# Linear attention and two squared-ReLU layers on one core: whole-word keys times values for the second token block, and split operands kept in two places

## The chip, the cores and the metric

The kernel runs on one core of a Trainium2 chip. The metric is device time in microseconds (us) of one execution; a median is taken over several.

## The reference

All tensors are float32; 8 batches, 8 heads, 576 positions, 64 values per head, so 4608 tokens of 512 values.

```python
q_s = softmax(q, over the 64 values of a head)
k_s = softmax(k, over the 576 positions)
kv  = einsum('bhsd,bhse->bhde', k_s, v)          # 64 x 64 for each batch and head
x   = einsum('bhsd,bhde->bhse', q_s, kv)         # then 4608 x 512
x   = (relu(x @ w_in)  ** 2) @ w_out             # 512 -> 2048 -> 512
y   = (relu(x @ w_in2) ** 2) @ w_out2            # 512 -> 2048 -> 512
```

## The kernel before, in words

**Tiling.** The tokens are cut into nine blocks of 512 (`j` = 0 to 8), the heads into four pairs (`p` = 0 to 3), the 2048 hidden values into sixteen chunks (`f`). There are four stages: the first layer's first product together with the attention (0 to some 500 us), its second product, and the two products of the second layer. The last three use a scheme with seven block products instead of eight and are not touched.

**Split operands.** Most products run in a reduced type. An operand is split into a high word (a copy by ScalarE) and a low word (operand minus high word, by VectorE), and a product takes three passes: low times high, high times low, high times high (`passes`, line 451; for the attention `x_mm`, line 411). A product in whole words, plain float32, needs no split.

**Attention.** Batches have 576 positions and blocks 512 tokens, so block `j` needs two batches: its first 64 `j` columns belong to batch `j` - 1, the rest to batch `j`. For a pair, keys are exponentiated, `kv_mm` (line 318) multiplies keys and values into the PSUM tile `kvps`, `kv_norm` (line 335) divides into `kvn`. `kv_hi` (line 343, ScalarE) and `kv_lo` (line 348, VectorE) write the two words of the pair's block-diagonal operand into `kvbd`. There is one `kvbd` for each pair, so `x_mm` comes in two parts: part 0 uses the words of batch `j` - 1, then `kv_hi` and `kv_lo` overwrite them, then part 1 uses batch `j`. The queries become probabilities, are transposed by VectorE into `qT` (`q_turn`, line 400) and split into `qhl` (`q_hi`, `q_lo`, lines 404 to 409). The result `xps` is split again into `xs` (`x_hi`, `x_lo`), which the first layer reads.

**Block 0** is the start and goes another way: keys and queries are transposed by TensorE against a unit matrix, `kv_whole0` (line 354) copies `kvn` whole into the tile `begin`, and `x_mm0` (line 295) multiplies in whole words. Batch 0's split words are still made, for block 1.

**Weights.** `first_weights` (line 764) brings in the sixteen weight chunks of the first product: a load, then `low_word`, `high_word`, `scaled` and `join` (lines 144 to 161) turn 64-bit numbers into float32, and `w_hi`, `w_lo` split them. `background` (line 823) converts the other three matrices during the first stage and later, one half chunk at a time, through a single room `qa`, by the same function `converted` (line 741).

**The order of the work** is written out by a planner in the kernel. Each step is an `op` with an engine, a cost in ns, a due time, the steps it follows, and the places (rooms of memory) that it uses. `schedule` (line 614) plays this through: on each engine the ready step with the earliest due time goes next, if its places are free. A place with one slot goes from user to user in the order in which they were written; `kvn`, `qT`, `qd` (which holds `begin`, then each `qhl` in turn) have one slot. `lag` is time added before a step counts as ready after a step of another engine. The instructions are then issued in that order, and each engine works through its own queue in order. `attend` (line 861) writes the steps of a block's attention, `plain_chunk` (line 939) those of a chunk of h.

Of the kernel before, what the change touches and what calls it, by code (L numbers as in the profile page):

```python
# [44 lines left out]
def linear_attention_two_relu2_ffn(ctx: ExitStack, tc: tile.TileContext, q0, k0, eye, qh, kh, vh, wio, out):  # L45
# [171 lines left out]
    kvbd = []  # L217
# [45 lines left out]
    def k_turn0(p, b1, b2):  # L263
        k = kt[0, p]
        a, b = ka[p] = wide(b1, f"ka{p}").rearrange("p (c n) -> p c n", n=P), wide(b2, f"kb{p}")
        for c in range(KC):
            r = slice(c * P, (c + 1) * P) if c < KC - 1 else slice(S - P, S)
            nc.tensor.transpose(a[:, c] if c < KC - 1 else b[:, :P], k[:, r], begin[1])
# [15 lines left out]
    def q_turn0(p, b):  # L284
        q = qt.pop((0, p)).rearrange("p a b -> p (a b)")
        ps = ka[p, "q"] = wide(b, f"qps{p}")
        for c in range(4):
            r = slice(c * P, (c + 1) * P)
            nc.tensor.transpose(ps[:, r], q[:, r], begin[1])
# [5 lines left out]
    def x_mm0(p, b):  # L295
        xps[0, p] = wide(b, f"xps0_{p}")
        nc.tensor.matmul(xps[0, p], begin[0][:, p], qTt.pop((0, p)), start=True, stop=True)
# [44 lines left out]

    def kv_hi(b, p):
        for j in range(2):
            r = slice(j * D, (j + 1) * D)
            nc.scalar.activation(out=kvbd[p][r, 0, r], in_=kvn[b, p][r], func=AF.Copy)

    def kv_lo(b, p):
        n, t = kvn.pop((b, p)), kvbd[p]
        for j in range(2):  # L350
            r = slice(j * D, (j + 1) * D)
            nc.vector.tensor_tensor(out=t[r, 1, r], in0=n[r], in1=f32(t[r, 0, r]), op=ALU.subtract)
# [104 lines left out]

    def filler(place, n):

        ps, z = bank(place, f"filler{place.index}")[:, 0], kvbd[0]  # L460
        for _ in range(n):
            nc.tensor.matmul(ps, z[:, 0], z.rearrange("p a n -> p (a n)"), start=True, stop=True)
# [101 lines left out]
    WORDS = {"qx": 2 * TB, "att1": KC * (P + 2 * (D + 1)), "att2": KC * (P + 2 * (D + 1))}  # L564
# [176 lines left out]
    def converted(f, a, h, due, raw, wf):  # L741
# [3 lines left out]
        c = op("ACT", act(512) + 40, due - 3000, lambda: low_word(f, a, h), [l], [rp])  # L745
        g = op("DVE", 430, due - 2900, lambda: high_word(f, a, h), [l], [rp], port=True)
# [435 lines left out]
```

## Time and profile before

| | us |
|---|---|
| median of 3 runs | 1543.55 (1541.88 to 1543.83) |
| the profiled execution's own time | 1544.59 |
| its span, first to last instruction | 1542.8 |
| TensorE matmuls busy | 1508.4 (98%) |
| VectorE busy | 1166.9 (76%) |
| ScalarE busy | 946.9 (61%) |
| GpSimd busy | 401.6 (26%) |
| mean granted TensorE clock | 0.99 |

In the profile PE is TensorE's matmuls, PEld its weight loads, DVE VectorE, ACT ScalarE, POOL GpSimd, SPq the queue that issues DMAs. On a timeline a row has the start in us, the length in us, the engine, the line, the operation, output <- inputs, shapes and how many instructions are merged; in brackets stands how long the engine had been idle before it, and what it waited for. Matmuls overlap, so lengths of neighbouring rows may add up to more than the time that passed.

### The profile page before, as it was taken

The page shows a single profiled execution, that of the slowest core. Times are in us where ns is not written, and L with a number is a line of the kernel's source. Part 1 is how long each engine was busy: PE and PEld are TensorE (multiplying, and loading weights), DVE is VectorE, ACT ScalarE, POOL GpSimd, SP SyncE. Part 2 cuts the span into 40 slices and gives each one's busy share as a digit, 9 for nine tenths or more (in the row PEclk, how much of TensorE's full clock was granted, in tenths as well). Part 3 has the DMA queues.
Part 4 walks back from the last instruction along what each step waited for, and adds up shares of the span by engine and source line. Part 5 has one row for each costly group of instructions (what it writes and reads, how often), then busy time and mean ns, then how long its engine had stood idle before and what let it go on. Part 6 is the DMA issues. An engine that isn't in the chain of part 4 may idle for free.

```text
span 1542.8 us, 29813 instructions
## 1 busy us (share of the span) xinstructions
PE 1508.4 (98%) x11664; PEld 1416.3 (92%) x11664; DVE 1166.9 (76%) x1694; ACT 946.9 (61%) x1605; POOL 401.6 (26%) x339
## 2 busy tenths in 40 slices
PE   6989999999999999999999999999999999999998
PEld 4777878888888999999999999999999999999998
DVE  7987868777723899999999644545356999999986
ACT  7876766766644666666655678878677544444332
POOL 2000000000103233333333533333312343333331
PEclk8999999999999999999999999999999999999999
DMA  9557779988644454444438767767448644444432
GB/s 347 175 181 246 256 230 322 315 299 288 223 142 158 138 170 140 143 137 140 141 115 339 248 210 254 257 214 263 151 171 299 231 141 138 138 143 132 141 117 69
DMA packets 143677, 307.18 MB, mean 199 GB/s; under 512 B 12592, under 2 KB 72112, under 8 KB 141488
## 3 DMA queue, kind: packets, MB, share of 16 engines
q1 hardware_dynamic: 142096, 286.93, 56.0%
q0 software_dynamic: 1440, 18.35, 3.2%
q8 instruction: 91, 1.49, 0.4%
q14 instruction: 50, 0.41, 0.1%
HBM read 179.93 MB, written 125.30 MB: 198 GB/s over the span
## 4 chain that ended last, share of the span: by engine, by line
PE 86%; DVE 5%; ACT 4%; DMA 3%; issue 1%; SPq 0%; DVEq 0%; ACTq 0%
PE y L455 43%; PE m L455 22%; PE h L455 19%; DMA raw<-wio 1%; PE kvps L324 1%; DMA w<-wf 1%; DVE G L118 1%; ACT wf L155 1%; DVE wf L160 1%; ACT w L146 0%; PE xps L419 0%; PE xps L418 0%; DMA qc<-w 0%; DMA att<-kh 0%; PE xps L417 0%
## 5 line engine op out<-in xcount | busy, mean ns | idle before, releaser
L455 PE MATMUL h<-hl,w 128*128 128x512 f32 x1620 | 391.7, 397 | 1.5 <-DVE w L80 1.5
L455 PEld LDWEIGHTS h<-hl,w 128*128 128x128 f32 x1620 | 304.4, 191 | 66.3 <-DVE w L80 1.6
L455 PE MATMUL m<-x,W 128*128 128x256 f32 x3024 | 345.8, 277 | 0.9 <-ACT ts L488 0.9
L455 PEld LDWEIGHTS m<-x,W 128*128 128x128 f32 x3024 | 345.2, 188 | 1.1 <-ACT ts L488 1.1
L455 PE MATMUL y<-W,G 128*128 128x256 f32 x3024 | 343.7, 276 | 0.6 <-DVE G L118 0.6
L455 PEld LDWEIGHTS y<-W,G 128*128 128x128 f32 x3024 | 343.3, 188 | 0.8 <-DVE G L118 0.8
L455 PE MATMUL y<-G,W 128*128 128x256 f32 x3024 | 343.3, 276 | 0.0
L455 PEld LDWEIGHTS y<-G,W 128*128 128x128 f32 x3024 | 343.2, 188 | 0.1
L113 ACT ACTIVATE G<-hl 128x512 fp32r<-128x512 f32 (+1 forms) x90 | 82.4, 929 | 103.3 <-PE y L455 61.6
L491 POOL TENSOR_TENSOR ts<-ts,ts 128x512 f32<-128x512 f32 x53 | 84.4, 1592 | 181.1 <-ACT ts L488 151.3
L118 DVE TENSOR_TENSOR G<-hl,G 128x512 fp32r<-128x512 f32 (+1 forms) x90 | 108.3, 1209 | 14.6 <-ACT G L113 14.4
L442 ACT ACTIVATE r<-h 128x512 f32<-128x512 f32 x144 | 85.0, 591 | 53.3 <-PE h L455 44.1
L500 DVE TENSOR_TENSOR t<-m,ts 128x512 f32<-128x512 f32 x72 | 48.8, 688 | 90.6 <-PE m L455 58.4
L309 POOL PARTITION_ALL_REDUCE m<-m x28 | 23.0, 820 | 347.8 <-DVE m L305 227.5
L506 ACT ACTIVATE t<-t 128x512 f32<-128x512 f32 x144 | 88.3, 627 | 2.0
L118 DVE TENSOR_TENSOR G<-att,G 128x1280 fp32r<-128x1280 f32 x50 | 81.1, 1623 | 10.2 <-ACT G L113 10.1
L118 DVE TENSOR_TENSOR G<-cf,G 128x1280 fp32r<-128x1280 f32 x52 | 81.1, 1560 | 8.8 <-ACT G L113 8.8
L503 ACT ACTIVATE t<-t 128x512 f32<-128x512 f32 x72 | 44.8, 629 | 43.3 <-DVE t L500 42.8
L113 ACT ACTIVATE G<-cf 128x1280 fp32r<-128x1280 f32 x52 | 65.7, 1264 | 8.0 <-DVE cf L100 8.0
L533 POOL TENSOR_TENSOR t<-t,t 128x512 f32<-128x512 f32 x34 | 59.5, 1769 | 27.5 <-DVE t L500 27.5
L113 ACT ACTIVATE G<-att 128x1280 fp32r<-128x1280 f32 x50 | 63.1, 1263 | 4.8 <-DVE att L100 4.8
L113 ACT ACTIVATE G<-qd 128x512 fp32r<-128x512 f32 x32 | 20.3, 633 | 68.0 <-PE y L455 40.3
(185 smaller groups left out, 1945.1 us busy)
## 6 DMA issues: line engine op xcount, KB each, us to landing
g<-r SPq DMA_DIRECT2D x144, 256.0 KB, 3.6
g<-t SPq DMA_DIRECT2D x144, 256.0 KB, 3.3
raw<-wio SPq DMA_DIRECT2D x48, 512.0 KB, 5.0
hl<-g SPq DMA_DIRECT2D x48, 512.0 KB, 3.8
y<-t SPq DMA_DIRECT2D x72, 256.0 KB, 2.4
W<-o POOLq DMA_DIRECT2D x10, 1792.0 KB, 10.1
qc<-g SPq DMA_DIRECT2D x32, 512.0 KB, 3.8
qd<-g SPq DMA_DIRECT2D x32, 512.0 KB, 3.6
```

Of the source, the lines that this page charges most:

```text
L113: nc.scalar.activation(out=hls[key][:, 0, r], in_=src, func=AF.Copy)
L118: nc.vector.tensor_tensor(out=hl[:, 1, r], in0=src, in1=f32(hl[:, 0, r]), op=ALU.subtract)
L155: nc.scalar.activation(out=part_w(f, a, h), in_=high, func=AF.Prelu, scale=2.0 ** -112, alpha=2.0 ** 32)
L160: nc.vector.scalar_tensor_tensor(out=u, in0=u, scalar=3, in1=low, op0=ALU.logical_shift_left, op1=ALU.bitwise_or)
L309: nc.gpsimd.partition_all_reduce(m[:, 1, :P], m[:, 0, :P], P, bass.bass_isa.ReduceOp.max)
L442: nc.scalar.activation(out=r0[j, f].rearrange("p a b -> p (a b)"), in_=m.pop(("h", j, f)), func=AF.Relu)
L455: nc.tensor.matmul(ps, a, b, start=start, stop=True, skip_group_check=True)
L491: nc.gpsimd.tensor_tensor(out=t[k, "s5"], in0=t[k, "s5"], in1=t[k, "s2"], op=ALU.add)
L500: nc.vector.tensor_tensor(out=temp(k, q), in0=m[k, i], in1=t[k, "s5"], op=ALU.add)
L503: nc.scalar.activation(out=t[k, q], in_=t[k, q], func=AF.Relu)
L506: nc.scalar.activation(out=t[k, q], in_=t[k, q], func=AF.Square)
L533: nc.gpsimd.tensor_tensor(out=t[k, q], in0=t[k, q], in1=t[k, o], op=ALU.add)
```

## The change

Block 1 now does as block 0: its products take whole words, from `begin[0][p]` (batch 0) and `begin[1][p]` (batch 1), with no split of its queries. From block 2 on there are two sets of split words, `kvbd[0]` and `kvbd[1]`, used by turns, the second in the rooms `hl0` and `hl1`; both parts of a product are one step. Batch 0's split words are no longer made; batch 1's are made from `begin[1]` after block 1's product. The unit matrix's quarter of the tile is blanked by GpSimd after the last transpose and becomes pair 3's place of `begin[1]`. Conversions of weights other than the first product's get a lag of 2500 ns. Some planner costs change. An unused helper is dropped.

```diff
+    def kv_of(b, p, r):
+        return begin[1][p][r, r] if b == 1 else kvn[b, p][r]
+
     def kv_hi(b, p):
         for j in range(2):
             r = slice(j * D, (j + 1) * D)
-            nc.scalar.activation(out=kvbd[p][r, 0, r], in_=kvn[b, p][r], func=AF.Copy)
+            nc.scalar.activation(out=kvbd[b % 2][p][r, 0, r], in_=kv_of(b, p, r), func=AF.Copy)
...
-    def kv_whole0(p):
+    def kv_whole(b, p):
         for j in range(2):
             r = slice(j * D, (j + 1) * D)
-            nc.scalar.activation(out=begin[0][r, p, r], in_=kvn[0, p][r], func=AF.Copy)
+            nc.scalar.activation(out=begin[b][p][r, r], in_=kvn[b, p][r], func=AF.Copy)
...
-    def x_mm(j, p, part, place):
-
-        if part == 0:
-            xps[j, p] = wide(place, f"xps{j}_{p}")
-        r = slice(0, D * j) if part == 0 else slice(D * j, TB)
-        ps, q, w = xps[j, p], qst[j, p], kvbd[p]
-        nc.tensor.matmul(ps[:, r], w[:, 1], q[:, 0, r], start=True, stop=False)
-        nc.tensor.matmul(ps[:, r], w[:, 0], q[:, 1, r], start=False, stop=False)
-        nc.tensor.matmul(ps[:, r], w[:, 0], q[:, 0, r], start=False, stop=True)
+    def x_mm(j, p, place):
+        ps = xps[j, p] = wide(place, f"xps{j}_{p}")
+        if j == 1:
+            q = qTt.pop((j, p))
+            for r, w in ((slice(0, D), begin[0][p]), (slice(D, TB), begin[1][p])):
+                nc.tensor.matmul(ps[:, r], w, q[:, r], start=True, stop=True)
+            return
+        q = qst[j, p]
+        for r, w in ((slice(0, D * j), kvbd[(j - 1) % 2][p]), (slice(D * j, TB), kvbd[j % 2][p])):
+            if r.start < TB:
+                nc.tensor.matmul(ps[:, r], w[:, 1], q[:, 0, r], start=True, stop=False)
+                nc.tensor.matmul(ps[:, r], w[:, 0], q[:, 1, r], start=False, stop=False)
+                nc.tensor.matmul(ps[:, r], w[:, 0], q[:, 0, r], start=False, stop=True)
...
+        late = 2500 if f else 0
+        c = op("ACT", act(512) + 40, due - 3000, lambda: low_word(f, a, h), [l], [rp], lag=late)
+        g = op("DVE", 430, due - 2900, lambda: high_word(f, a, h), [l], [rp], lag=late, port=True)
...
-            nm = op("DVE", 600, d - 6000, lambda: kv_norm(0, p), [kvmm], [s, n, ps])
-            wh = op("ACT", 500, d - 5000, lambda: kv_whole0(p), [nm, start_eye], [n, beginroom])
-            hi = op("ACT", 500, d + 8000, lambda: kv_hi(0, p), [nm, kv_zero], [n, kvp[p]])
-            kv_ready[p] = op("DVE", 450, d + 9000, lambda: kv_lo(0, p), [hi], [n, kvp[p]], port=True)
-            xlast = op("PE", 1300, d - 3000, lambda: x_mm0(p, xb), [wh, qe], [xb, qT, beginroom])
+            nm = op("DVE", 640, d - 6000, lambda: kv_norm(0, p), [kvmm], [s, n, ps])
+            wh = kv_done[0, p] = op("ACT", 500, d - 5000, lambda: kv_whole(0, p), [nm, start_eye], [n, beginroom])
+            xlast = op("PE", 1150, d - 3000, lambda: x_mm0(p, xb), [wh, qe], [xb, qT, beginroom])
...
-            y = op("ACT", act(512), d - 10500, lambda: q_hi(j, p), [y], [qd, qT])
-            qe = op("DVE", dve(512), d - 9000, lambda: q_lo(j, p), [y], [qd, qT], port=True)
-            xlast = xm = op("PE", 60 + 3 * 29 * j, d - 7500, lambda: x_mm(j, p, 0, xb), [qe, kv_ready[p]], [xb, qd, kvp[p]], lag=SLACK)
             if own:
-                nm = op("DVE", 600, d - 8500, lambda: kv_norm(j, p), [kvmm], [s, n, ps])
-                hi = op("ACT", 500, d - 6500, lambda: kv_hi(j, p), [nm, xm], [n, kvp[p]])
-                kv_ready[p] = op("DVE", 450, d - 5500, lambda: kv_lo(j, p), [hi], [n, kvp[p]], port=True)
-                xlast = op("PE", 60 + 3 * 29 * (8 - j), d - 4500, lambda: x_mm(j, p, 1, xb), [kv_ready[p], xm], [xb, qd, kvp[p]], lag=SLACK)
+                nm = op("DVE", 640, d - 8500, lambda: kv_norm(j, p), [kvmm], [s, n, ps])
+            if j == 1:
+                wh = op("ACT", 500, d - 7500, lambda: kv_whole(1, p), [nm, start_eye, blank[0]], [n, beginroom])
+                xlast = op("PE", 1250, d - 5500, lambda: x_mm(1, p, xb), [y, wh, kv_done[0, p]], [xb, qT, beginroom], lag=SLACK)
+                hi = op("ACT", 500, d + 1000, lambda: kv_hi(1, p), [wh, kv_zero], [beginroom, kvp[1][p]])
+                kv_ready[1, p] = op("DVE", 450, d + 2000, lambda: kv_lo(1, p), [hi], [beginroom, kvp[1][p]], port=True)
+            else:
+                y = op("ACT", act(512), d - 10500, lambda: q_hi(j, p), [y], [qd, qT])
+                qe = op("DVE", dve(512), d - 9000, lambda: q_lo(j, p), [y], [qd, qT], port=True)
+                if own:
+                    hi = op("ACT", 500, d - 7500, lambda: kv_hi(j, p), [nm, kv_zero, x_done[j - 1, p]], [n, kvp[j % 2][p]])
+                    kv_ready[j, p] = op("DVE", 450, d - 6500, lambda: kv_lo(j, p), [hi], [n, kvp[j % 2][p]], port=True)
+                xlast = op("PE", 1200, d - 5500, lambda: x_mm(j, p, xb), [qe, kv_ready[j - 1, p], kv_ready.get((j, p))], [xb, qd, *(kvp[i % 2][p] for i in (j - 1, j) if i < B)], lag=SLACK)
+            x_done[j, p] = xlast
...
+    def blank_unit():
+        blank[0] = op("POOL", 300, -8000, lambda: nc.gpsimd.memset(unit[0], 0.0), turned, [beginroom])
...
-        r = pool.tile([P, NP + 1, P], F32, name="begin", tag="qd")
-        begin[:] = r[:, :NP], r[:, NP]
-        nc.sync.dma_start(out=begin[1], in_=eye)
-        nc.gpsimd.memset(begin[0], 0.0)
+        r = pool.tile([P, 2 * NP, P], F32, name="begin", tag="qd")
+        begin[:] = [r[:, p] for p in range(NP)], [r[:, NP + (p + 1) % NP] for p in range(NP)]
+        unit.append(r[:, NP])
+        nc.sync.dma_start(out=unit[0], in_=eye)
+        nc.gpsimd.memset(r[:, :NP], 0.0)
+        nc.gpsimd.memset(r[:, NP + 1:], 0.0)
...
-            nc.gpsimd.memset(f32(t[:, p]), 0.0)
-            kvbd.append(t[:, p])
-
-    kv_zero = op("POOL", 800, 0, zeros, [], kvp)
+            kvbd[0].append(t[:, p])
+            kvbd[1].append(xspace[p // 2].area(WIDE + 6 * TB + 2 * P * (p % 2), 2 * P, F32R).rearrange("p (a n) -> p a n", a=2))
+        for t in (*kvbd[0], *kvbd[1]):
+            nc.gpsimd.memset(f32(t), 0.0)
+
+    kv_zero = op("POOL", 1200, 0, zeros, [], [*kvp[0], *kvp[1]])
```

## Rows read from the trace of the kernel before

**Rows 1.** The page's busy times, and two lines of TensorE's waits (total, times, longest).

```profile
PE 1508.4 (98%) x11664; PEld 1416.3 (92%) x11664; DVE 1166.9 (76%) x1694; ACT 946.9 (61%) x1605; POOL 401.6 (26%) x339
...
PE xps L417 <- DVE kvbd L352: 4.1, 2, 2.3
PE xps L297 <- ACT begin L357: 3.9, 2, 2.2
```

**Rows 2.** Stretches: length, PE, PEld, DVE, ACT, POOL busy, clock, DMA share, GB/s.

```profile
30.00:85.00 55.00, 51.31 (x274) 40.47 (x275) 50.01 (x116) 47.33 (x114) 4.40 (x5) 0.93 0.62 199
...
88.53:98.15 9.62, 5.48 (x50) 3.88 (x48) 8.38 (x24) 6.97 (x18) 1.44 (x2) 0.69 0.40 125
98.15:149.00 50.85, 50.85 (x278) 41.85 (x276) 40.73 (x92) 34.92 (x86) 2.11 (x3) 0.99 0.75 238
...
236.30:503.70 267.40, 267.40 (x1422) 220.02 (x1423) 171.39 (x360) 164.69 (x366) 30.82 (x31) 1.00 0.72 245
```

**Rows 3.** VectorE's timeline at the opening: the tile kvn changes hands.

```profile
28.45 0.46 DVE L352 TENSOR_TENSOR kvbd<-kvn,kvbd 64x64 fp32r<-64x64 f32 x2
...
29.93 0.28 DVE L341 TENSOR_SCALAR kvn<-kvps,kvs 128x64 f32<-128x64 f32 x1
```

**Rows 4.** Timelines of GpSimd and TensorE at the opening, to the first chunk of h.

```profile
0.73 1.05 POOL L1124 MEMSET kvbd<- 128x256 f32 x4 [0.29 <-POOLq L1174]
...
22.25 0.95 PE L324 MATMUL kvps<-w,att 128*64 128x65 f32 x20 [1.66 <-ACT att L273]
...
30.89 2.07 PE L297 MATMUL xps<-qx,begin 128*128 128x512 f32 x2 [2.23 <-ACT begin L357]
31.97 9.79 PE L455 MATMUL h<-hl,w 128*128 128x512 f32 x36
```

**Rows 5.** TensorE's timeline: a product in whole words, a second part in three passes.

```profile
15.72 1.10 PE L297 MATMUL xps<-qx,begin 128*128 128x512 f32 x2 [0.44 <-issue]
...
88.53 0.37 PE L417 MATMUL xps<-qhl,kvbd 128*128 128x448 f32 x1
...
89.24 0.95 PE L324 MATMUL kvps<-att 128*64 128x65 f32 x20
```

**Rows 6.** TensorE's timeline in blocks 0 and 1: waits, and 24 matmuls of h.

```profile
66.49 0.30 PE L418 MATMUL xps<-qhl,kvbd 128*128 128x64 f32 x1 [1.28 <-DVE qhl L80]
...
68.41 7.27 PE L455 MATMUL h<-hl,w 128*128 128x512 f32 x24 [1.51 <-DVE w L80]
...
77.10 5.74 PE L455 MATMUL h<-hl,w 128*128 128x512 f32 x24
...
98.15 6.12 PE L455 MATMUL h<-hl,w 128*128 128x512 f32 x24
```

**Rows 7.** Timelines of VectorE and ScalarE: pair 3 of block 1.

```profile
79.34 0.70 DVE L402 STREAM_TRANSPOSE qT<-qx 128x512 f32<-128x512 f32 x1
...
85.84 0.28 DVE L341 TENSOR_SCALAR kvn<-kvps,kvs 128x64 f32<-128x64 f32 x1
...
90.95 0.63 ACT L77 ACTIVATE qhl<-qT 128x512 fp32r<-128x512 f32 x1
...
94.74 0.46 DVE L352 TENSOR_TENSOR kvbd<-kvn,kvbd 64x64 fp32r<-64x64 f32 x2
```

**Rows 8.** VectorE's timeline: low words of the sixteenth weight of the first product.

```profile
84.85 0.69 DVE L80 TENSOR_TENSOR hl<-wf,hl 128x512 fp32r<-128x512 f32 x1
```

**Rows 9.** Timelines around the two holes in blocks 2 to 4.

```profile
150.71 0.68 ACT L146 ACTIVATE raw<-raw 128x512 uint32<-128x512 uint32 x1 [1.97 <-DMA raw<-wio]
...
152.06 0.95 PE L324 MATMUL kvps<-att 128*64 128x65 f32 x20 [2.93 <-ACT att L316]
152.94 7.40 PE L455 MATMUL h<-hl,w 128*128 128x512 f32 x24
...
231.30 0.38 PE L417 MATMUL xps<-qhl,kvbd 128*128 128x256 f32 x1 [1.83 <-DVE kvbd L352]
...
231.75 4.50 PE L455 MATMUL h<-hl,w 128*128 128x512 f32 x12
```

More of the change, by code (lines that the diff above doesn't have):

```diff
@@ L214, in w_lo @@
         lo_of(w0[f], wfs.pop((0, f % NPAIR, f // NPAIR)).rearrange("p a n -> p (a n)"))
-    kvbd = []
+    kvbd = [[], []]
     kt, vt, qt, mt, qmt, qTt, qst, kvps, xps = ({} for _ in range(9))
@@ L267, in k_turn0 @@
             r = slice(c * P, (c + 1) * P) if c < KC - 1 else slice(S - P, S)
-            nc.tensor.transpose(a[:, c] if c < KC - 1 else b[:, :P], k[:, r], begin[1])
+            nc.tensor.transpose(a[:, c] if c < KC - 1 else b[:, :P], k[:, r], unit[0])
     def k_out0(p, new):
@@ L288, in q_turn0 @@
             r = slice(c * P, (c + 1) * P)
-            nc.tensor.transpose(ps[:, r], q[:, r], begin[1])
+            nc.tensor.transpose(ps[:, r], q[:, r], unit[0])
     def q_out0(p, new):
@@ L296, in x_mm0 @@
         xps[0, p] = wide(b, f"xps0_{p}")
-        nc.tensor.matmul(xps[0, p], begin[0][:, p], qTt.pop((0, p)), start=True, stop=True)
+        nc.tensor.matmul(xps[0, p], begin[0][p], qTt.pop((0, p)), start=True, stop=True)
     def k_max(b, p, place):
@@ L345, in kv_hi @@
             r = slice(j * D, (j + 1) * D)
-            nc.scalar.activation(out=kvbd[p][r, 0, r], in_=kvn[b, p][r], func=AF.Copy)
+            nc.scalar.activation(out=kvbd[b % 2][p][r, 0, r], in_=kv_of(b, p, r), func=AF.Copy)
     def kv_lo(b, p):
-        n, t = kvn.pop((b, p)), kvbd[p]
+        t = kvbd[b % 2][p]
         for j in range(2):
             r = slice(j * D, (j + 1) * D)
-            nc.vector.tensor_tensor(out=t[r, 1, r], in0=n[r], in1=f32(t[r, 0, r]), op=ALU.subtract)
-    def kv_whole0(p):
+            nc.vector.tensor_tensor(out=t[r, 1, r], in0=kv_of(b, p, r), in1=f32(t[r, 0, r]), op=ALU.subtract)
+    def kv_whole(b, p):
         for j in range(2):
             r = slice(j * D, (j + 1) * D)
-            nc.scalar.activation(out=begin[0][r, p, r], in_=kvn[0, p][r], func=AF.Copy)
+            nc.scalar.activation(out=begin[b][p][r, r], in_=kvn[b, p][r], func=AF.Copy)
     qmo, qso = {}, {}
@@ L456, in passes @@
                 start = False
[L458 to L462, printed above, removed]
     m, t, t_place = {}, {}, {}
@@ L855, in linear_attention_two_relu2_ffn @@
     kvroom = Place("qe")
-    kvp = [Place(f"kvbd{p}", parent=kvroom) for p in range(NP)]
-    kv_ready, x_ready, x_place = {}, {}, {}
     qspace = Place("qx")
     xspace = [Place("hl0"), Place("hl1")]
+    kvp = [[Place(f"kv{i}_{p}", parent=xspace[p // 2] if i else kvroom) for p in range(NP)] for i in range(2)]
+    kv_ready, kv_done, x_done, x_ready, x_place = {}, {}, {}, {}, {}
+    turned = []
     def attend(j, p):
@@ L887, in attend @@
                 ke = op("ACT", act(640), d - 11500, lambda: k_exp(j, p), [y], [kp])
-                kvmm = op("PE", 1200, d - 10000, lambda: kv_mm(j, p, ps), [ke], [ps, kp], lag=SLACK)
+                kvmm = op("PE", 960, d - 10000, lambda: kv_mm(j, p, ps), [ke], [ps, kp], lag=SLACK)
         xb = Place("ps")
@@ L934, in linear_attention_two_relu2_ffn @@
             plan(when(0, j) - 25000 - (3 - p) * 12500, lambda j=j, p=p: attend(j, p))
+        if j == 0:
+            plan(when(0, 0) - 25000, blank_unit)
     stored, y_stored = {}, {}
@@ L1087, in linear_attention_two_relu2_ffn @@
             plan(when(2, j) - (24000 if j == 0 else 11000) + 5000 * kk, lambda j=j, kk=kk: between(j, kk))
-    begin = [None, None]
+    begin, unit = [[], []], []
     beginroom = Place("qd")
```

16 lines of the change are left out of this document (9 added, 7 removed).

## The prediction

> **What bounds the kernel now.** I read the page first, then the table of waits, then the stretches by stage, and only then single instructions on the timelines. The page's first lines [rows 1] say that TensorE is busy 98% of the span and every other engine less: the span is TensorE's work plus its holes. So the question is which holes a change to the attention can reach. The waits view [rows 1] names two releasers in the changed code: the low words of `kvbd` (line 352) and the whole copy into `begin` (line 357). The stretches [rows 2] place the largest hole between blocks 0 and 1: from 88.53 to 98.15 us TensorE is busy 5.48 of 9.62 us at a granted clock of 0.69; from 236 to 503 us there is none. The timelines add the opening, a place in block 0, and two in blocks 2 to 4. In the same stretches VectorE is nearly full up to the first boundary (50.01 of 55 us from 30 to 85) and has air afterwards (40.73 of 50.85, then 171.39 of 267.4). This second fact limits the gain.
>
> **The change, part by part.**
>
> **The opening.** One tile `kvn` carries every pair's normalised product, and the next pair's may be written only when the last reader is done. In block 0 that last reader is the low-word subtraction (line 352), which serves block 1. The pair that ended at 28.45 + 0.46 us was followed at once by the last pair's normalisation, written at 29.93 [rows 3], although that pair's multiplication had ended at 22.25 + 0.95 = 23.20 [rows 4]. TensorE waited 3.9 us in two pieces for such copies [rows 1], and its last product took 2.07 us [rows 4]. The change drops high and low words of block 0's kv altogether; `kvn` is free after the whole copy. From 23.20 the three outstanding products, 1.1 us each [rows 5], could follow directly, so the first chunk of h could start at 26.5 instead of 31.97: **-5.5**. Bounds: 0 if the first weights aren't there, 7 if the last multiplication moves up too; I take the value that the row of the multiplication gives.
>
> **Inside block 0.** TensorE waited 1.28 us for pair 1's low query words and 1.51 us for a weight, and the 24 matmuls after it took 7.27 us where 24 others took 5.74 [rows 6]: 1.28 + 1.51 + 1.53 = **-4.3** if both waits go (0 if none does). The query words of block 1 are no longer split.
>
> **Between blocks 0 and 1.** Here sits a serial chain. The split query words have one tile, `qhl`; a pair's second part frees it, and only then can the next pair begin; between its two parts lie high and low words of kv. Pair 3's transposed queries were there at 79.34 + 0.70, but their split began at 90.95, and the kv words for its second part at 94.74 [rows 7]. After the change a pair needs only the transposed tile and the whole-word kv, so pair 3 can be multiplied while block 0 still runs. Useful work in the 9.62 us was about 3.4: two last parts of 0.71 [rows 5], two multiplications of 0.9 for block 2, 0.2 for a first part. That leaves 6.2, and 0.4 for the next 24 matmuls at lower clock (6.12 against 5.74): **-6.6**. Bounds 0 and 6.6.
>
> **What the product costs.** In block 1 three reduced passes become whole-word products. The whole-word product of 512 columns takes 1.10 us; three reduced passes over 448 columns took 0.71 (88.53 to 89.24), so 0.81 for 512 [rows 5]. Four pairs: **+1.2**. That a second, 64-column piece has a cost of its own isn't shown for this type; bounds 0 and, if it cost a whole product, 4.4. I take 1.2, since the reduced passes are priced by their columns.
>
> **Other engines.** ScalarE loses four query copies and four kv pairs of copies and gains four whole copies; it is not the last to arrive at these places. GpSimd's extra memsets (four blocks, the rest of the starting tile, the blanked unit matrix) stand in its idle time. Four blocks of 256 columns took 1.05 us [rows 4], so these 1536 columns some 1.6, and that is what they cost if the first query subtraction had to wait for them. The blanking waits for the last transpose with the unit matrix, which stands ahead of the multiplication at 22.25 [rows 4], long before block 1's first whole copy. The starting tile now keeps the `qd` room until block 1's words are split; block 2's split queries queue behind it, as block 1's did before.
>
> **VectorE's limit.** The three gains need weights, and the weights come through VectorE: the last of block 0's sixteen was ready at 84.85 + 0.69 = 85.54 [rows 8]. Before it VectorE sheds four kv subtractions of 0.46 and four query subtractions of 0.69 (4.6 us), and takes in 1.3 us that used to come later (a normalisation and a subtraction of block 1): 82.2. With all of its 5.0 idle us filled it would be 77.2. One chunk of 2.87 us later block 1 can start: 80.1 to 85.1. TensorE's own sum is 26.5 + 56.6 (31.97 to 88.53) - 4.3 + 1.2 + 1.6 (products that move into the block) = 81.6. I take 83. Against 98.15 that is 15.1; two multiplications of block 2 that stood in the hole come later (1.8), and the 0.4 of clock is gained: **-13.7** for everything up to there.
>
> **The later holes.** At 152.06 TensorE waited 2.93 us for an exponential that stood in ScalarE's queue behind a weight load still on its way (ScalarE sat 1.97 us before it), and the next 24 matmuls took 7.40 instead of 5.74. At 231.30 it waited 1.83 us for the kv words before a second part, and 12 matmuls took 4.50 instead of 2.87 [rows 9]. Together 4.6 + 3.5 = 8.1. The new lag puts such conversions later in the order, and the halves of a product no longer wait for each other. It makes the one weight room turn slower, which VectorE's air to 503 us covers [rows 2]. I take **-6.0**: a changed order brings a hole of its own somewhere. Bounds 0 and -8.1.
>
> Of those sums 5.2 us are clock, not waiting: 1.5, 0.4, 1.7 and 1.6, each the same matmuls at the lower of the two levels (1.2 and 2.4 GHz) after a wait. The Trainium skill, TensorE: Matmul & The Clock Gate, "What's actually happening", speaks against counting them: for modelling it calls the ramp under 1% of a span, and says not to fit it. By that rule the sum would be some 5 us smaller, about 1529; by the rows it stays, since three separate waits each show about 1.5.
>
> **Sum.** -13.7 - 6.0 = -19.7. The profiled execution took 1544.59 us (1.8 around its span), so 1524.9. It lies 1.0 above the median of the runs shown: **1524**.
>
> **The rivals.**
>
> *VectorE sets block 0 as before.* Nothing of its idle time is filled, the earlier start only makes TensorE wait for weights in the middle, and the clock falls there. Block 1 starts at 85.1 or a little later; with 1.5 us of clock that is about -9, and the later holes are replaced by others. 1544.6 - 9 - 1 = 1534.6. For it: 50 of 55 us busy [rows 2]. Against: part of the idle time is waiting inside the chain that goes away. Chance 0.20.
>
> *The hole moves one boundary on.* In the hole VectorE did 8.38 us [rows 2], of which 1.8 finished block 1 (two subtractions of 0.69, one of 0.46) and 6.6 prepared what follows. That now has to fit into block 1. If it doesn't, block 2 starts 6.6 us late, with 1.5 of clock: -19.7 + 8.1 = -11.6, so 1532. Against: 10 us of air in block 1 [rows 2], and the chain of a pair is shorter there too. Chance 0.13.
>
> *Slower: the loads without a lag.* Keys, values and queries are still planned to land as before, and no hole is left in front of blocks 2 to 8 to absorb a late one. The place is the head of ScalarE's or VectorE's queue, the price 4.6 us each [rows 9]. Two such holes (8.1 us) are in the present time. With 13.7 gained, the balance turns beyond (13.7 + 8.1) / 4.6 = 4.7 of them; one at each of seven boundaries gives 1544.6 - 13.7 - 8.1 + 32.2 - 1 = 1554. Against: in the present trace one such exponential is late, behind a load that now has the lag. Chance 0.08.
>
> *The change doesn't reach the hole.* If pair 3's keys times values, not its queries, were late, the opening would still gain and the rest cancel: within the noise. Against: its `kvn` was written at 85.84 [rows 7], before the hole. Chance 0.04.
>
> **How the numbers follow.** The forecast has the remaining 0.55. Its own range is 1518 (every hole gone: 1544.6 - 1 - 16.4 + 1.2 - 8.1 = 1520, and 2 for a shorter opening) to 1530. The whole range goes on to 1538, past the first two rivals. Faster or slower means by over 0.2%, 3.1 us, about what a measurement of this kernel can tell from no change. Faster: 0.55 + 0.20 + 0.13, less 0.01 = 0.87. Same 0.05, slower 0.08.
>
> **What would show it.** Right: the first chunk of h near 26.5 us; no wait of an `xps` product for `kvbd` in block 1; block 1's first chunk near 83 instead of 98.15; no kv multiplication waiting for an exponential near 140 us. Wrong: a row of waits of h for `w` from VectorE between 45 and 80 us (first rival), a low granted clock near 135 us (second), several `kvps` waits behind `att` (third), or a wait at the same place for another releaser.

## The result, and the profile after

The changed kernel took 1529.26 us in the median of 4 runs (1528.46 to 1530.54), the kernel before 1542.97 (1541.88 to 1543.83): a ratio of 0.9912, 95% interval 0.9895 to 0.9929. The forecast was 1524 in a range of 1517 to 1538. The direction holds and the time lies in the range, 5 us above the forecast; one large step of the sum failed, and a rival's sign showed. The profiled execution took 1529.49 us with a span of 1527.7. Of some of the kernels below, and of the kernel before, a part of the executions is some 11 us longer, in the two of them that were profiled all of it in the last stage; times are then given for the shorter group, ratios over all.

The page of the changed kernel, busy times (which answer to [rows 1]):

```profile
PE 1503.2 (98%) x11656; PEld 1411.5 (92%) x11656; DVE 1164.7 (76%) x1682; ACT 947.4 (62%) x1601; POOL 408.3 (27%) x345
```

The totals hardly move; the gain can't be seen here. The stretches of the first stage show it. Columns as in [rows 2]: stretch, length, busy time of PE, PEld, DVE, ACT, POOL, then clock, DMA share, GB/s. The kernel before, cut at its own milestones (first chunk of h, end of block 0, block 1, second stage):

```profile
0.00:31.97 31.97, 17.23 (x124) 10.54 (x125) 24.99 (x61) 24.22 (x54) 5.88 (x13) 0.87 0.96 365
31.97:88.53 56.56, 53.76 (x289) 42.77 (x288) 51.50 (x120) 47.27 (x113) 4.40 (x5) 0.95 0.58 185
...
149.00:503.50 354.50, 349.59 (x1861) 286.28 (x1858) 237.26 (x506) 221.59 (x500) 36.17 (x37) 0.99 0.73 247
sum 503.50, PE 476.90 PEld 385.32 DVE 362.87 ACT 334.96 POOL 49.99; mean PE 95.38 PEld 77.06 DVE 72.57 ACT 66.99 POOL 10.00
```

The changed kernel, the same way; it has no stretch between blocks 0 and 1:

```profile
0.00:26.05 26.05, 16.23 (x125) 10.54 (x125) 19.36 (x46) 18.66 (x40) 7.43 (x19) 0.98 0.94 355
26.05:90.80 64.75, 57.50 (x290) 43.96 (x289) 56.50 (x128) 53.33 (x129) 4.47 (x5) 0.93 0.55 198
90.80:149.00 58.20, 58.20 (x342) 47.48 (x341) 49.91 (x119) 42.81 (x112) 5.49 (x5) 1.00 0.74 237
149.00:488.80 339.80, 339.80 (x1833) 278.65 (x1832) 239.63 (x495) 220.86 (x487) 39.32 (x37) 1.00 0.76 256
sum 488.80, PE 471.73 PEld 380.63 DVE 365.40 ACT 335.65 POOL 56.71; mean PE 117.93 PEld 95.16 DVE 91.35 ACT 83.91 POOL 14.18
```

The second stage starts 14.7 us sooner (503.50 to 488.80), and from there on the two kernels take the same 1039 us. Of the 14.7, TensorE's idle time gives 9.5 (503.5 - 476.9 = 26.6, against 17.1) and its busy time 5.2 (476.9 against 471.7): nearly the same matmuls, more of them at the higher clock. From 90.80 us on TensorE has no hole in this stage. But block 0, from its first chunk of h to its last, has become longer: 64.75 us against 56.56, with 7.25 us of idle time in it against 2.80. With the hole behind it [rows 2] the kernel before took 66.18 us from there to block 1, 6.94 of them idle. So the idle time has moved from the boundary into block 0; it has not shrunk.

What TensorE waited for in all, in the changed kernel (total, times, longest):

```profile
PE h L462 <- DVE w L80: 7.3, 4, 2.4
...
PE xps L297 <- ACT begin L360: 2.0, 2, 1.5
```

The wait of products for `kvbd` [rows 1] has left the list; the wait of h for weights has grown from 1.5 us in one place to 7.3 in four. On TensorE's timeline of the changed kernel (start, length, what; in brackets the idle time before it and its releaser):

```profile
19.97 0.95 PE L324 MATMUL kvps<-w,att 128*64 128x65 f32 x20 [0.45 <-ACT att L273]
...
22.04 1.13 PE L297 MATMUL xps<-qx,begin 128*128 128x512 f32 x2 [0.53 <-ACT begin L360]
24.67 1.97 PE L297 MATMUL xps<-qx,begin 128*128 128x512 f32 x2 [1.50 <-ACT begin L360]
...
51.09 2.99 PE L462 MATMUL h<-hl,w 128*128 128x512 f32 x12 [1.37 <-DVE w L80]
...
57.64 7.38 PE L462 MATMUL h<-hl,w 128*128 128x512 f32 x24 [2.32 <-DVE w L80]
...
68.27 4.57 PE L462 MATMUL h<-hl,w 128*128 128x512 f32 x12 [2.37 <-DVE w L80]
72.68 1.14 PE L419 MATMUL xps<-qT,begin 128*128 128x64 f32 x4
75.00 2.97 PE L462 MATMUL h<-hl,w 128*128 128x512 f32 x12 [1.19 <-DVE w L80]
...
78.78 5.75 PE L462 MATMUL h<-hl,w 128*128 128x512 f32 x24
84.36 1.14 PE L419 MATMUL xps<-qT,begin 128*128 128x64 f32 x4
...
88.08 2.20 PE L462 MATMUL h<-hl,hl 128*128 128x512 f32 x9
90.12 0.84 PE L462 MATMUL h<-hl 128*128 128x512 f32 x3
90.80 2.88 PE L462 MATMUL h<-hl,w 128*128 128x512 f32 x12
93.61 0.95 PE L324 MATMUL kvps<-att 128*64 128x65 f32 x20
```

The last chunk of block 0 (the two rows without `w`: its weight, too, stands in a place `hl`) runs to 90.80, and block 1's first chunk follows at once: the hole of [rows 2] is gone. Inside the block there are four waits for weights, and after the two longer ones the same matmuls took 7.38 us instead of 5.75, and 4.57 instead of 2.97: 3.2 us at a lower clock.

Why do the weights come late? The shortest of the four waits shows the engines waiting for each other in turn, at 72 to 75 us. ScalarE's timeline there, in the changed kernel:

```profile
72.88 0.60 ACT L449 ACTIVATE r<-h 128x512 f32<-128x512 f32 x1 [2.24 <-PE h L462]
73.50 0.63 ACT L211 ACTIVATE w<-wf 128x512 fp32r<-128x512 f32 x1
```

and VectorE's:

```profile
74.16 0.69 DVE L80 TENSOR_TENSOR w<-wf,w 128x512 fp32r<-128x512 f32 x1 [1.68 <-ACT w L211]
...
86.78 0.68 DVE L80 TENSOR_TENSOR hl<-wf,hl 128x512 fp32r<-128x512 f32 x1
```

ScalarE's next step in its queue is the copy of a finished chunk (`r`), for which it waits 2.24 us; behind it in the queue stands the high word of the next weight; VectorE waits 1.68 us for that word, and TensorE 1.19 us for VectorE.

The longest wait, of 2.37 us up to 68.27, shows the order itself. First ScalarE's row, then VectorE's:

```profile
64.54 0.63 ACT L211 ACTIVATE w<-wf 128x512 fp32r<-128x512 f32 x1
...
65.05 0.69 DVE L401 TENSOR_TENSOR qx<-qx,qs 128x512 f32<-128x512 f32 x1
65.66 0.68 DVE L385 TENSOR_TENSOR qx<-qx,qm 128x512 f32<-128x512 f32 x1
66.26 0.70 DVE L405 STREAM_TRANSPOSE qT<-qx 128x512 f32<-128x512 f32 x1
...
67.44 0.68 DVE L80 TENSOR_TENSOR w<-wf,w 128x512 fp32r<-128x512 f32 x1
```

The high word of the weight was there at 64.54 + 0.63 = 65.17. VectorE's low words for it started 2.3 us later, behind steps of block 1's attention; TensorE used the `qT` made there only at 72.68.

The last weight's low words come at 86.78, later than the 84.85 of [rows 8], although VectorE has less to do. VectorE was busy 47.90 of the 55 us from 30 to 85 us, against 50.01 before [rows 2]:

```profile
30.00:85.00 55.00, 47.75 (x254) 36.15 (x252) 47.90 (x112) 45.94 (x114) 4.47 (x5) 0.94 0.55 195
```

### The profile page after: what moved, and what is told of

It reads as the page before. It is cut to its first block, busy times and chain, and to the rows that moved or that the text cites. A ratio compares the mean times of both kernels' runs of the same rounds, so it can differ in the third digit from the quotient of the medians.

```text
span 1527.7 us, 29799 instructions
## 1 busy us (share of the span) xinstructions
PE 1503.2 (98%) x11656; PEld 1411.5 (92%) x11656; DVE 1164.7 (76%) x1682; ACT 947.4 (62%) x1601; POOL 408.3 (27%) x345
## 4 chain that ended last, share of the span: by engine, by line
PE 94%; DVE 3%; ACT 2%; issue 1%; DMA 0%; DVEq 0%; SPq 0%; ACTq 0%
PE y L462 43%; PE h L462 25%; PE m L462 23%; PE kvps L324 2%; DVE G L118 1%; PE xps L426 0%; PE xps L425 0%; PE xps L424 0%; ACT w L146 0%; ACT wf L155 0%; ACT w L211 0%; ACT r L449 0%; DMA w<-k 0%; ACT w L256 0%; DVE w L80 0%
```

## The experiments

Each run gives two figures: its time, and the start of the second stage in the profiled execution (before 503.5, changed 488.8). The second is the cleaner one. I name the kernels of the experiments by what they differ in.

**The late release of kvn, alone.** The kernel before, in which only the due times of batch 0's two split words move, so that they stand before the next pair's normalisation instead of long behind it:

```diff
-            hi = op("ACT", 500, d + 8000, lambda: kv_hi(0, p), [nm, kv_zero], [n, kvp[p]])
-            kv_ready[p] = op("DVE", 450, d + 9000, lambda: kv_lo(0, p), [hi], [n, kvp[p]], port=True)
+            hi = op("ACT", 500, d - 4900, lambda: kv_hi(0, p), [nm, kv_zero], [n, kvp[p]])
+            kv_ready[p] = op("DVE", 450, d - 4800, lambda: kv_lo(0, p), [hi], [n, kvp[p]], port=True)
```

> The kernel before with two due times changed and nothing else: the split of batch 0's kv words (lines 902 and 903) is due right after the whole copy instead of 8 to 9 us past the block's time, so that the one tile kvn is released early as in the changed kernel. If kvn alone delayed the opening (theory of the prediction), the first chunk of h starts at 27 to 30 us instead of 32. For the boundary of blocks 0 and 1 two theories differ: by the prediction the serial chain of the split query words makes the hole, so block 1 still starts near 98 us and the time falls by at most 2 (1541 to 1543); if instead the late kvn started the delay that the chain only hands on, block 1 starts near 91 us, as in the changed kernel, and the time is 1535 to 1538.

Measured: ratio 0.9962 (0.9931 to 0.9993), 10 runs spread from 1533.66 to 1550.16 (8 of them up to 1540.94); first chunk of h at 29.20, within what was expected; block 1 at 94.90, halfway between the two theories, so that neither fits; second stage at 497.63, 5.9 earlier. TensorE's timeline of this kernel around the boundary:

```profile
85.72 5.98 PE L455 MATMUL h<-hl,w 128*128 128x512 f32 x24
91.54 0.37 PE L417 MATMUL xps<-qhl,kvbd 128*128 128x448 f32 x1
...
94.22 0.84 PE L455 MATMUL h<-hl 128*128 128x512 f32 x3
94.90 2.88 PE L455 MATMUL h<-hl,w 128*128 128x512 f32 x12
```

and its waits for weights:

```profile
PE h L455 <- DVE w L80: 7.4, 5, 2.2
```

The boundary's hole is gone, with `qhl` and `kvbd` still in one place each; in its stead h waits 7.4 us for weights inside block 0, as in the changed kernel. Block 1's start makes 3.2 of the 5.9 us; the rest went from the later holes.

**The lag, alone.** The kernel before, with the change's lag on the conversions and nothing else:

```diff
-        c = op("ACT", act(512) + 40, due - 3000, lambda: low_word(f, a, h), [l], [rp])
-        g = op("DVE", 430, due - 2900, lambda: high_word(f, a, h), [l], [rp], port=True)
+        c = op("ACT", act(512) + 40, due - 3000, lambda: low_word(f, a, h), [l], [rp], lag=2500 if f else 0)
+        g = op("DVE", 430, due - 2900, lambda: high_word(f, a, h), [l], [rp], lag=2500 if f else 0, port=True)
```

> The kernel before with the lag of 2500 ns alone, nothing else of the change. Theory A (the lag removes the two later holes): 8.1 us less, 1535 (1533 to 1537), with the hole from 88.5 to 98.2 us unchanged. Theory B (the joined products with two places do it): the second hole, a wait for kv words between two parts of a product, stays; between 1538 and 1543. A third way, that the lag only moves the holes: 1543 within 2.

Measured: 8 of 10 runs between 1535.35 and 1536.81; ratio 0.9951 (0.9924 to 0.9979); second stage at 495.23, 8.3 earlier. The holes of [rows 9] are gone, in this stretch of that kernel:

```profile
125.00:495.00 370.00, 370.00 (x2013) 302.97 (x2013) 256.50 (x550) 239.80 (x536) 37.84 (x39) 1.00 0.76 252
```

The boundary's hole stays (2.5 us of waiting for `kvbd`, 1.4 for `qhl`; block 1 at 97.16).

**The change without its lag** (`late = 0`).

```diff
-        late = 2500 if f else 0
+        late = 0
```

> The changed kernel with its 2500 ns of lag on the weight conversions taken back, all else as changed. The holes at 152 and 231 us of the kernel before were worth 8.1 us (4.6 and 3.5), and the changed kernel has none after block 0. If the lag removed them (theory A), holes of about that size come back in blocks 1 to 4: 1529.3 + 8, so 1534 to 1538, with waits of a kv multiplication behind an exponential that stands behind a weight load. If the joined products with two places removed them (theory B), the time stays at 1529.3 within 1.5. In both cases blocks 0 and 1 start as in the changed kernel, at 26.05 and 90.80.

Measured: 1528.45 (1528.02 to 1529.3), ratio 0.9892 (0.9857 to 0.9928); second stage at 487.37, as theory B had it. No later hole came back: beside the joined product and the two places the lag adds nothing. Blocks 0 and 1 start at 25.61 and 89.37, not at 26.05 and 90.80 as was expected, so the lag changes the order there too. Either of the two is enough, but neither is needed: the last version below has neither, and no later hole.

**The change with block 1 split as before**: two places, the joined product and the lag stay; whole words only in block 0.

```diff
+            hi = op("ACT", 500, d + 8000, lambda: kv_hi(0, p), [nm, kv_zero], [n, kvp[0][p]])
+            kv_ready[0, p] = op("DVE", 450, d + 9000, lambda: kv_lo(0, p), [hi], [n, kvp[0][p]], port=True)
...
-            if j == 1:
-                wh = op("ACT", 500, d - 7500, lambda: kv_whole(1, p), [nm, start_eye, blank[0]], [n, beginroom])
-                xlast = op("PE", 1250, d - 5500, lambda: x_mm(1, p, xb), [y, wh, kv_done[0, p]], [xb, qT, beginroom], lag=SLACK)
...
```

> The changed kernel with block 1 taken back to split words: batch 0's and 1's kv words split from kvn, block 1's queries split, its product in three passes, but two places for the kv words by turns, both parts as one step, and the lag. If the whole words of block 1 make the gain at the first boundary (chain of the split queries), block 1 starts near 98 us again and the time is 1536 to 1540; if the two places do it, block 1 starts near 91 to 94 us and the time is 1530 to 1533. The first chunk of h should start near 30 us rather than 26, since kvn is held by batch 0's split again.

Measured: 7 of 10 runs between 1531.48 and 1534.04; ratio 0.9929 (0.9895 to 0.9963); first chunk of h at 30.25, block 1 at 92.97, second stage at 490.96. Whole words in block 1 (with batch 0's split words dropped) bring 2.2 us of the second stage's start; they come from the opening, which they make 4.2 us earlier, and block 0 gives half of that back.

**Is it VectorE, or ScalarE?** In the changed kernel the low words, or else the high words, of the last eight weights of the first product are written twice (the same values), 5.5 us more for VectorE, or 5.0 for ScalarE, inside block 0 (the planner's cost of these steps is doubled with them). The two edits, one in each kernel:

```diff
-        lo_of(w0[f], wfs.pop((0, f % NPAIR, f // NPAIR)).rearrange("p a n -> p (a n)"))
+        src = wfs.pop((0, f % NPAIR, f // NPAIR)).rearrange("p a n -> p (a n)")
+        for _ in range(2 if f >= 8 else 1):
+            lo_of(w0[f], src)
...
-        nc.scalar.activation(out=w0[f][:, 0], in_=wfs[0, f % NPAIR, f // NPAIR].rearrange("p a n -> p (a n)"), func=AF.Copy)
+        for _ in range(2 if f >= 8 else 1):
+            nc.scalar.activation(out=w0[f][:, 0], in_=wfs[0, f % NPAIR, f // NPAIR].rearrange("p a n -> p (a n)"), func=AF.Copy)
```

> The changed kernel with VectorE's subtraction for the low word made twice for the last eight weights (the second writes the same values again): 8 x 0.69 = 5.5 us more for VectorE before block 1, nothing more for ScalarE. If VectorE's throughput sets the end of block 0, as the prediction has it, block 1 starts 4 to 5.5 us later than 90.80; if ScalarE's does, 0 to 1.5 us later; in the ring of waits about as much as the run with the copy twice.

> The changed kernel with ScalarE's copy of the high word made twice for the last eight weights of the first product (the second writes the same values again): 8 x 0.63 = 5.0 us more for ScalarE before block 1, nothing more for VectorE. If ScalarE's throughput sets the end of block 0, block 1 starts 4 to 5 us later than 90.80; if VectorE's does, 0 to 1.5 us later; if neither is full and the engines wait for each other in a ring (chunk, result copy, weight word, next chunk), 2.5 us or more, since the copy stands in that ring.

Measured: low words twice 1529.72 and 1531.38 us, second stage at 489.05; high words twice 1529.03 and 1529.08, second stage at 487.94. Five us more of work on either engine cost 1.3 us at most. Neither the 4 us or more that were expected of a full engine nor the 2.5 expected of a ring of waits show at the second stage. The two stretches, first with low words twice, then with high words twice:

```profile
30.00:85.00 55.00, 46.10 (x246) 34.65 (x245) 49.82 (x112) 45.07 (x112) 3.46 (x4) 0.94 0.56 195
```

```profile
30.00:85.00 55.00, 48.41 (x256) 36.78 (x255) 48.85 (x114) 50.18 (x121) 4.47 (x5) 0.94 0.55 195
```

Of VectorE's 5.5 us only 1.9 show as more busy time in its stretch (49.82 against 47.90): other steps were put off in its favour. So the test doesn't show an engine with room for five us more; it shows that what an engine does before block 1 isn't fixed. (In these two the planner puts one chunk of block 1 ahead of block 0's last, so their block boundary isn't compared.)

**Is it the order?** The changed kernel, with the first product's weights from the fifth on due 8 us earlier, so that they stand ahead of block 1's attention in every queue:

```diff
-        d = when(0, 0, f) - 500
+        d = when(0, 0, f) - 500 - (8000 if f >= 4 else 0)
```

> The changed kernel with the weights 4 to 15 of the first product due 8 us earlier, nothing else. TensorE waits 7.3 us for weights in block 0 there and loses some 3 to 4 us more at the lower clock after these waits. If this is an order that puts block 1's attention ahead of weights that are needed first, the waits for weights go and block 1 starts 4 to 8 us earlier (83 to 87), so the time is 1521 to 1526. If VectorE and ScalarE simply have too much to do before block 1, the waits move to block 1's first chunk, for its last pair, and the time is 1528 to 1531.

Measured: 1522.42 (1522.09 to 1523.57), ratio 0.9834 (0.9787 to 0.9881); second stage at 480.96, 7.8 earlier than in the changed kernel. In its stretch, and in its waits:

```profile
30.00:85.00 55.00, 50.89 (x295) 38.63 (x294) 50.84 (x118) 48.90 (x122) 4.03 (x5) 1.00 0.61 210
```

```profile
PE h L462 <- DVE w L80: 3.8, 4, 1.7
```

No instruction was taken away. TensorE, VectorE and ScalarE each do some 3 us more in these 55 us than in the changed kernel (50.89, 50.84, 48.90 against 47.75, 47.90, 45.94), the granted clock is 1.00 against 0.94, and on this kernel's timeline block 1 starts at 83.94, after a wait of 0.47 us for an exponential and with all its weights there:

```profile
83.06 0.95 PE L324 MATMUL kvps<-att 128*64 128x65 f32 x20 [0.47 <-ACT att L316]
83.94 8.45 PE L462 MATMUL h<-hl,w 128*128 128x512 f32 x36
```

With the split words of block 1's kv moved into block 1 as well:

```diff
-                hi = op("ACT", 500, d + 1000, lambda: kv_hi(1, p), [wh, kv_zero], [beginroom, kvp[1][p]])
-                kv_ready[1, p] = op("DVE", 450, d + 2000, lambda: kv_lo(1, p), [hi], [beginroom, kvp[1][p]], port=True)
+                hi = op("ACT", 500, when(0, 1) + 2000, lambda: kv_hi(1, p), [wh, kv_zero], [beginroom, kvp[1][p]])
+                kv_ready[1, p] = op("DVE", 450, when(0, 1) + 2000 + 1000, lambda: kv_lo(1, p), [hi], [beginroom, kvp[1][p]], port=True)
```

> As the run with the weights first, and in addition the split of batch 1's kv words (four pairs, 2.1 us of ScalarE and 1.8 us of VectorE) is due after block 1's start instead of within block 0. If the two engines' work before block 1 is the bound, this gives another 1.5 to 2.5 us against that run; if not, the two runs agree within 1.

Measured: 1521.69 (1521.4 to 1523.36), ratio 0.9831 (0.9775 to 0.9887), second stage at 480.53. That can't be told from the version without it. Both are faster than the two kernels of the case.

**What do the small edits do without the new buffers?** Four more versions of the kernel before: the early words and the lag of the first two experiments together; the weights 8 us earlier alone (line 832 there, the same edit as above); all three; and the early words with the earlier weights.

> The kernel before with the two small edits together (the first block's split keys-times-values words due at d-4900 and d-4800, as in the change; and the 2500 ns of lag on the loads' word split), none of the new buffers, no whole words in block 1, no joined product. Theory A, the two gains are of separate places and add up: the two alone moved the second stage's first product from 503.5 us to 495.4 and to 497.8 (8.1 and 5.7 to 5.9 us), together 489.5 to 490, so 1529 to 1530.5 us, as fast as the changed kernel (1529.3), block 1's first chunk near 95 us and no idle of TensorE after 125 us. Theory B, they share a cause, or the whole words and the second place are needed for the rest: the second stage at 493 us or later, 1533 us or more.

> The kernel before with one edit: the first product's weights from the fifth on due 8 us earlier in the planner's order. Theory A, the order of the work sets the end of block 0 in the kernel before as in the changed one, but the pair's buffer between two blocks, which comes free late, still sets when block 1 starts: the last weight's low word some 4 to 6 us before 84.85, h(0,15) done by about 84 instead of 88.5, block 1's first chunk within 2 us of 98.15 all the same, a longer idle stretch at the boundary, and 1541 to 1544 us. Theory B, block 0's end carries through: block 1's first chunk at 91 to 93 us, 1535 to 1538 us. If the later holes stay (8 us), that is the same in both.

> The kernel before with all three small edits (early split words of the first block, the lag, the weights 8 us earlier), none of the new buffers. Theory A, the new buffers, the whole words in block 1 and the joined product carry nothing that the order doesn't: second stage at 481 to 483 us, 1522 to 1524 us, like the changed kernel with its weights first (1522.42). Theory B, with the weights first the attention of block 1 becomes late and its four-step chain (two split words more and one place for the split operands) stands open: idle time of TensorE between h(0,15) and block 1 of 3 to 8 us, second stage at 485 to 490 us, 1526 to 1530 us.

> The kernel before with two of the three small edits: the first block's split words early, and the weights from the fifth on 8 us earlier; no lag, none of the new buffers. Theory A, the second stage's opening hole of the version with all three (5.4 us of waits after 497 us) came from the order that the lag made, not from a want of the new buffers: here the second stage starts at 488 to 490 us as there (or 2 to 4 us later, where a late exponential stands without the lag), then runs without a wait, 1527 to 1531 us. Theory B, the hole comes with the weights due earlier or the early words: it is there again and the time is 1533 us or more. In both, block 1 starts near 90 us and not near 84 as in the changed kernel with its weights first: its pairs still wait for split words in one place, so the two places and the whole words are worth the 6 us between.

| version | us (runs) | ratio (95% interval) | block 1 starts | second stage starts |
|---|---|---|---|---|
| early words, lag | 7 of 10 runs 1531.43 to 1534.73 | 0.9958 (0.9932 to 0.9984) | 93.08 | 491.60 |
| weights first | 4 runs 1531.35 to 1532.43 | 0.9929 (0.9912 to 0.9945) | 91.18 | 491.13 |
| all three | 3 of 10 runs 1537.08 to 1537.53, the others 1548.24 to 1560.95 | 1.0005 (0.9971 to 1.0038) | 90.10 | 488.26 |
| early words, weights first | 6 of 10 runs 1529.68 to 1530.27 | 0.9939 (0.9905 to 0.9973) | 90.55 | 489.07 |

Early words and lag give 11.9 of the 14.1 us that their single gains add up to; that lies between the two expectations, so a small part of their gain is shared. The earlier weights alone brought the boundary forward by 7 us where theory A expected nothing of it: in the kernel before, too, it was largely the order that made the hole. The later holes, which both theories left in place, went as well: of their waits, 4.8 us [rows 9], two others of 0.54 and 0.92 are left. This one line took 11 us off the kernel before, against 13.7 for the whole change.

With all three the first stage ended where theory B put it (with 1.3 us of waiting at the boundary, not 3 to 8), but the time is 1537, not 1526 to 1530, since then the second stage's first operands came late, which none of the kernels above shows. TensorE's timeline of that version:

```profile
488.26 11.29 PE L455 MATMUL y<-G,W 128*128 128x256 f32 x96
501.49 0.38 PE L455 MATMUL y<-G,W 128*128 128x256 f32 x1 [1.94 <-ACT G L113]
503.26 5.34 PE L455 MATMUL y<-G,W 128*128 128x256 f32 x30 [1.39 <-DVE G L118]
...
512.31 7.87 PE L455 MATMUL y<-G,W 128*128 128x256 f32 x65 [1.66 <-DVE G L118]
```

Without the lag, and nothing else different, that hole was not there: 1530, as theory A had it. So it comes with the lag in that order, not from a want of buffers. Which of the reordered loads does it was not followed up. In that last version, which has neither lag nor joined product, nothing is left of the holes in blocks 2 to 4, so these too hang on the order:

```profile
125.00:488.00 363.00, 363.00 (x1967) 297.28 (x1966) 254.15 (x544) 235.19 (x531) 36.09 (x39) 1.00 0.76 257
```

Its pair 3's second part still waits for its kv words at the boundary:

```profile
86.57 0.28 PE L419 MATMUL xps<-qhl,kvbd 128*128 128x64 f32 x1
88.15 0.49 PE L417 MATMUL xps<-qhl,kvbd 128*128 128x448 f32 x1 [1.31 <-DVE kvbd L352]
```

It reaches block 1 at 90.55 and the second stage at 489.07; the changed kernel with its weights first is at 83.94 and 480.96. So the new buffers with the whole words (and a lag, which moved little on the changed kernel) are worth some 8 us once the weights come first. In the kernel's own order they are worth 2.8: 488.80 against the 491.60 of the version with early words and lag. Both figures include the changed planner costs (the multiplication of keys and values stands at 960 ns instead of 1200, for one), which all versions of the changed kernel have and none of the kernel before; no run takes them by themselves.

## Why the prediction was right or wrong

**The opening** (-5.5) came out in size, 31.97 to 26.05 being -5.9, but in part by luck. The forecast let three products follow the last multiplication, from 23.20 on, without a wait. In the changed kernel that multiplication ended at 19.97 + 0.95 = 20.92, 2.3 us sooner, and from there 5.1 us passed instead of 3.3, with waits of 0.53 and 1.50 us for `begin` in them (3.9 before). The release of `kvn` is the larger part of the cause: with `kvn` held again (two places) the first chunk of h is at 30.25, so 4.2 of the 5.9 us go with the release and the dropped words. That version has the sooner multiplication too, at 19.68, so this is not the release; what moved it, the changed planner costs perhaps, isn't shown.

**Between blocks 0 and 1** the hole went, as forecast, but its cause was told too narrowly. The prediction laid it on the single `qhl`; the early words alone close it with that tile unchanged, and the weights' order alone moves the boundary 7 us. The chain was where a delay from block 0's late `kvn` and from the queue order came out.

**VectorE's limit**, with **inside block 0**, is the step that failed: that the weights of block 0 and the attention of block 1 would both fit into what VectorE had idle before 83 us. It let block 1 start at 83, with the idle parts of VectorE partly filled and the two waits in block 0 gone; it started at 90.80. The waits did not go (-4.3): they became 7.3 us of waiting for weights, with 3.2 us of low clock behind them. Nor were the 6.6 us of the boundary's hole gained: from block 0's first chunk to block 1's the forecast left 56.5 us of 66.18, and it took 64.75, with as much idle time as before. The reason given, "the weights come through VectorE", took a busy share of 50 in 55 us for a limit of throughput. Five and a half us more of VectorE work moved the second stage by 0.25, and the same work in another order started block 1 at 83.94. What sets block 0's end is the order in the queues: attention of block 1 stands ahead of weights that are needed first (2.3 us of it at the longest wait), and the ring of waits at 72 to 75 us is the same at the shortest. The first rival (VectorE sets block 0 as before) had foretold the sign, waits of h for `w` from 45 us on with the clock falling, and put block 1 at 85.1 or a little later; it too gave VectorE's throughput as the reason, and its price came out otherwise, for it kept holes further on.

**The products** (+1.2) were mis-sized, and of the wrong sign. From 84.36 to 88.08 stand one product of block 1 and 12 matmuls of h; the next 12 took 93.61 - 90.80 = 2.81, so the product took 0.91, not the 1.10 of the opening. A second piece of 64 columns didn't cost a whole product; the upper bound of 4.4 falls. The other side, 0.81, was the 448 columns' 0.71 scaled to 512; but the kernel before does the 64 columns as a part of their own:

```profile
82.68 0.20 PE L417 MATMUL xps<-qhl,kvbd 128*128 128x64 f32 x1
...
82.94 3.01 PE L455 MATMUL h<-hl,w 128*128 128x512 f32 x12
85.79 2.23 PE L455 MATMUL h<-hl,hl 128*128 128x512 f32 x9
```

That part and 12 matmuls took 3.11 us, the part alone 0.30. Both parts came to about 1.0, so the four whole-word products gain some 0.4 instead of costing 1.2.

**The later holes** (-6.0, bound -8.1) went altogether, and no new one came. The discount for "a hole of its own somewhere" was taken in the wrong block. That the lag is what removes them is only half right: without it the change removes them as well, and so does another order with neither lag nor joined product.

**The sum** agrees better than its steps. Up to block 1's start the gain was 98.15 - 90.80 = 7.35, less 1.8 for the two multiplications moved and plus the 0.4 of clock, about -6.0 instead of -13.7; the later holes gave -8.1 instead of -6.0. Together -14.1 instead of -19.7; the span fell by 15.1. That the time lies within 5 us of the forecast is in part luck: 7.7 us of the first gain are missing, and 2.1 more from the later holes and 1.0 that no step accounts for make up for some of it.

**The rivals.** The second (a hole one boundary on) didn't happen: TensorE is busy 58.20 of 58.20 us from 90.80 to 149. Nor did the late loads: there is no wait of `kvps` for an exponential in blocks 2 to 8, even without the lag.

**The clock.** The Trainium skill's rule (TensorE: Matmul & The Clock Gate, "What's actually happening") that the clock's ramp is under 1% of a span and not to be fitted would, as the prediction read it, have given about 1529, and 1529 it is, but not on that ground: the 5.2 us of low clock that the prediction counted did go from their places, and 3.2 us came back behind two new waits. These 3.2 us are 0.2% of the span, which agrees with the rule, and a fifth of the change's effect.

## What to carry to other kernels

A queue that is nearly full over a stretch isn't thereby the limit: ask what stands in it ahead of the step that the bound engine waits for, and move that first; here one due time was worth 7 to 11 us. When a hole closes, look for the same wait earlier in the chain before counting the gain, since the work that arrives sooner meets whatever was second latest. And try parts of a change alone: here lag and buffers removed the same holes, and three changed due times took the kernel before to 1530, while the worth of the new buffers rose from 3 to 8 us once the order was right.

## What was not expected of the hardware

Not each wait cost clock, and its length doesn't tell which does. In the changed kernel the matmuls after waits of 1.37 and 1.19 us took 2.99 and 2.97 us for 12, as without a wait, and those after 2.32 and 2.37 lost 1.6 each; with the weights first, waits of 1.46 and 1.70 left the granted clock at 1.00 throughout. In the kernel before, 1.5 us were lost behind a wait of 1.51, which another of 1.28 had preceded [rows 6]. With the low words twice, a wait of 1.93 us was followed by 4.60 us for 12 matmuls, at a granted clock of 0.66 from 50 to 55 us, but a wait of 2.70 cost nothing, at 1.00 from 68 to 73:

```profile
69.19 3.01 PE L464 MATMUL h<-hl,w 128*128 128x512 f32 x12 [2.70 <-DVE w L80]
```

The whole-word product in block 1 (0.91 us) is no dearer than the three reduced passes in two parts that it replaces (about 1.0), where the opening's rows suggested a third more.

The matmuls of the last stage have two durations, 276 and 281 ns at the same granted clock and with the same tiles, over the stretch from 1300 to 1500 us: 281 in the profiled executions of the kernel before with the lag and of that with the early words, 276 in the others looked at. Nothing in those stretches waits. What sets it stays open.
